# Moving the mask's rows head by head and exchanging two ScalarE operations in a fused attention and FFN kernel

## The chip, the cores and the metric

The kernel runs on one core of one Trainium2 chip. The metric is the device time of one launch in microseconds (us). A core has five engines that run their own instruction lists in order and wait for one another by semaphores: TensorE (PE in the profile; PEld is its weight load), VectorE (DVE), ScalarE (ACT), GpSimd (POOL) and SyncE (SP), which in this kernel issues nearly all DMA transfers. A DMA instruction waits on its issuing engine until its inputs are ready and its target is free, and all that stands behind it on that engine waits with it.

## The reference

Attention over 4 x 8 heads of 768 tokens with 64 values each, in which a query sees only the keys of its own hash bucket, and then a feed-forward layer with a rational function between its two products.

```python
q_bits = (einsum('bhsd,dk->bhsk', q, proj) > 0)      # 6 bits; k_bits likewise
mask = q_bucket[:, :, :, None] == k_bucket[:, :, None, :]
scores = where(mask, q @ k.T / sqrt(64), -1e9)
scores = scores - max(scores)
attn = exp(scores);  attn = attn / (sum(attn) + 1e-9)
x = (attn @ v), heads side by side                    # 3072 tokens x 512
h = x @ w_in                                          # 512 -> 2048
P = a0 + a1*h + a2*h*h + a3*h*h*h
Q = 1 + |b0|*|h| + |b1|*h*h
out = (P / (Q + 1e-6)) @ w_out                        # 2048 -> 512
```

All numbers are float32.

## The kernel before

The 32 heads are worked on as 16 pairs, p = 0 to 15. A pair has twelve score steps (two halves of 384 queries, six tiles of 128 keys), and each step makes the scores of both heads. The order of nearly all work on every engine comes from one list written by hand: `at(p, s, f, ...)` puts a call at place 12 * p + s, and the calls run in the order of their places. Below, **window w** is the stretch from place 12 * w to 12 * w + 12, in which pair w's scores are made, and "step s" is a place within it. While window w makes the scores of pair w, it also prepares pair w + 2 (its mask and its row maxima) and finishes pair w - 1.

What one window holds, as far as the change touches it:

- `scores` (one at each whole step): on the TensorE two matmuls for each head (`pss`), and on ScalarE one exponential for each head (`E<-pss`). The results stand in PSUM tiles that three buffers serve in turn, so the fourth tile of a row of scores can only be written when ScalarE has read the first.
- `values`: 24 matmuls for a half of a pair (`psv`), which sum into a PSUM tile of which there is one. `values_col` and `values_out` are the two ScalarE operations that read this tile (`col<-psv`, `xo<-psv,col`), and `values_store` is the DMA that puts the result into DRAM (`x_d<-xo`). For the second half of pair p they stand at steps 0.5, 1.5 and 3.0 of window p + 1.
- `high` and `low` split q and k of pair p into two parts on ScalarE and VectorE; `high_move` (step 1.9 of window p - 2, DMAs `q<-q` and `k<-k`) moves half of the first part to the other head's tile, and `second_high` (step 2.69) issues four more DMAs of the same names for pair p - 1.
- `bits` makes, for two pairs at once and in every even window, the rows that carry the bucket mask (`psb` on the TensorE, `mb<-psb` on VectorE); `penalties` scales them on ScalarE in place (`mb<-mb,cst`), at step 4.02.
- `maskrows` (step 4.03 of window p - 2) moves those rows by DMA into rows 64 to 76 of pair p's q and k tiles: `q<-mb` and `k<-mb` for head 0, then the same for head 1. For one of q's two tiles and one of k's, these are rows that `high_move` reads from, so the first of them has to wait for that DMA's end. In even windows it also waits for `penalties`.
- `maxstep` (twelve, from step 6.54 of window p - 2; `psm` on the TensorE, `m<-psm` on VectorE) makes the row maxima with those rows in the operands; the first six are head 0's. `shift_turn` (`pst`, `mt<-pst`) and `shift_rows` (`q<-mt`) turn the maxima into one more row of q.
- `load` (step 4.04) fetches q and k of a later pair (`qkf<-qT`, `qkf<-kT`, 384 KB each), and `weights` fetches and splits the FFN's weights (`wr<-w_in`, `wr<-w_out`, 512 KB each) along the way.

Window 0 has places of its own (the table `FIRST`): the mask's rows of pair 2 are moved at 8.2, both heads together, behind `penalties` at 7.315; the rows of the shift of pair 1 at 8.6 and 14.35; the load of pair 4 is at 7.35 (`load4`).

The FFN comes after the attention, from about 384 us on.

Of the kernel before, what the change touches and what calls it, by code (L numbers as in the profile page):

```python
# [21 lines left out]
NT = S // P  # L22
# [3 lines left out]
NPAIR = B * NHP  # L26
# [15 lines left out]
MID = dict(  # L42
    group=6, values=[0.66, 0.05], values_col=[1.5, 1.5], values_out=[2.5, 2.5],
    maxima=[6.54, 7.17, 8.32, 9.1, 10.1, 11.02, 12.25, 13.03, 14.15, 15.17, 16.01, 17.02], sums=17.05, sums_store=18.9,
    high=[-0.975, -0.974], low=[-0.946, 3.3, 3.35], bits=-0.945, penalties=4.02, high_move=1.9, maskrows=4.03, second_low=-2.2,
    second_high=2.69, load_v=10.99, shift_turn=5.67, shift_rows=8.82, load=4.04, recips=[23.5, 35.02, 35.3],
    weights=[[1.44, 5.01, 5.015, 5.06, 5.07, 5.08, 5.09, 5.3], [8.05, 11.005, 11.006, 11.022, 11.023, 11.024, 11.0255, 11.0256, 19.32, 21.22]],
    late_weights=[[1.44, 5.1, 5.11, 5.5, 5.65, 5.66, 11.02, 11.023], [8.05, 11.021, 11.022, 11.022, 11.024, 11.0245, 17.05, 17.665, 19.32, 21.22]],
    defer={5: 11.0252, 10: 17.1, 11: 17.2}, early_load=4.035, early_store=16.034, weights_last=[0.5, 0.8, 1.0, 1.2],
)  # L50

FIRST = dict(
    maxima1=[-0.072, -0.05, 5.52, 5.97, 6.42, 6.87, 7.32, 7.77, 8.22, 8.67, 9.12, 9.57], maxima2=9.5, rate2=0.82, high=[3.25, 3.53],
    low=[6.0, 6.05], bits=7.31, penalties=7.315, high_move=4.53, maskrows=8.2, second_low=-24.19, second_high=4.35, load_v=4.78, group=2,
    values=[-1.07, 2.65, 2.32, 2.35, 0.35, 0.61], values_out=3.02, high1=[-3.0, -3.2], low1=[-2.8, -2.95],
    high_move1=-2.7, load2=-2.6, load3=3.8, load4=7.35, penalties1=-24.26, maskrows1=-24.2,
    weights=[[-27.25, 5.45, 5.455, 6.9, 6.91, 7.317, 17.55, 18.3], [7.34, 9.04, 9.23, 9.24, 9.25, 9.26, 9.3, 11.9, 12.5, 46.81]],
    warm0=9, warm1=1, warm=3, warms=[3, 3, 3, 0, 1, 0], maxima00=[-4.3, -2.3, -4.2, -0.9, -1.2, -0.8], shift00=[-1.0, -0.2],
    shift0=[-0.08, -0.075], ahead=3, scores=[[-0.85, -0.4, -0.1], [0.1, 0.3, 0.4]], pen01=[-2.9, -0.35],
    second_high0=[-3.42, -3.4, -3.3, -3.25], load_v0=-3.3, bits1=-0.3, comp1=[-0.28, -0.27],  # L60
# [6 lines left out]
LAST = dict(  # L67
    group=6, values=[0.28, 0.44], values_out=0.46, vout14=[3.5, 3.03],
    hi14=17.05, weights15=[5.1, 5.11],
    tokens=[[-15.0, -11.5, -8.6, -4.9], [-7.43, -4.5, -2.83, -1.09], [1.1, 4.2, 5.45, 6.3]], terms=1.0, ffn=[13.61, 16.09, 16.14],  # L70
    sums=16.96, wide=8, share=6, third=0, sums14=14.69, weights14=-1.0, load_v=1.5, sumst14=22.46,
)
# [31 lines left out]
def move(nc, out, in_, queue=None):  # L104

    (queue or nc.sync).dma_start(out.bitcast(F32), in_.bitcast(F32))
# [72 lines left out]
def attention(ctx, tc, nc, raw, ps_b, tail, tokens, early, operands_to_terms, ffn, load, QF, KF, v, w_in, w_out, wo_d, ident, cst, ones, prj,  # L179
# [32 lines left out]
    Q1, Q2, K1, K2, LO, V, M, MB, ACC, EXP, AV, MS = ({} for _ in range(12))  # L212
# [51 lines left out]
        rows = MB[p + which[0]][0][sl]  # L264
        nc.scalar.activation(rows, rows.bitcast(F32), AF.Identity, scale=cst[sl, 1:2])

    def maskrows(p, queues=(None, None)):
        mb, o = MB.pop(p)
        for h in range(2):
            o1 = o + 14 * h  # L270
            move(nc, Q1[p][64:76, h, :], mb[o1 : o1 + 12].rearrange("p f c -> p (f c)"), queues[0])
            move(nc, K1[p][64:77, h, :], mb[o1 + 32 : o1 + 45].rearrange("p f c -> p (f c)"), queues[1])
# [228 lines left out]
    def at(p, s, f, *args):  # L501
        plan.setdefault(12 * p + s, []).append((f, args))
# [5 lines left out]
    for p in range(NPAIR):  # L508
        mid = 0 < p < NPAIR - 1
        n = MID["group"] if mid else (FIRST if p == 0 else LAST)["group"]  # L510
        for s in range(12):
            if p > 0 or s >= FIRST["ahead"]:
                at(p, FIRST["steps"].get(s, s) if p == 0 else s, scores, p, s)

            if p > 1:
                at(p - 2, FIRST["maxima2"] + FIRST["rate2"] * s if p == 2 else FIRST["third"] if p == 3 and s == 0 else MID["maxima"][s], maxstep, p, s, None, p == 2 or s not in MID["defer"])
                if p > 2 and s in MID["defer"]:
                    at(p - 2, MID["defer"][s], maxreduce, p, s)
            if s % n == n - 1:
                for i in range(s - n + 1, s + 1):  # L520
                    at(p, s + (MID["values"][s // n] if mid else (FIRST if p == 0 else LAST)["values"][s // n]), values, p, i)
            if s % NT == NT - 1 and mid and p < NPAIR - 2:
                at(p, s + MID["values_col"][s // n], values_col, p, s // NT)
            if s % NT == NT - 1:
                at(p, s + (LAST["vout14"][s // NT] if p == NPAIR - 2 else MID["values_out"][s // n] if mid else (FIRST if p == 0 else LAST)["values_out"]), values_out, p, s // NT)
        for hf in range(2):
            at(p, 6 * hf + 9, values_store, p, hf)
        if p < NPAIR - 1:
            at(p, MID["sums"] if p < NPAIR - 2 else LAST["sums14"], sums, p)
            at(p, MID["sums_store"] if p < NPAIR - 2 else LAST["sumst14"], sums_store, p)  # L530
        if p > 1:
            for t in range(2):
                at(p - 2, (MID if p > 2 else FIRST)["high"][t], high, p, t)
                at(p - 2, (MID if p > 3 else FIRST3)["low"][t + t * p % 2] if p > 2 else FIRST["low"][t], low, p, t, nc.vector if p > 3 else nc.gpsimd)
            if p % 2 == 0:
                at(p - 2, (MID if p > 2 else FIRST)["bits"], bits, p)
                at(p - 2, (MID if p > 2 else FIRST)["penalties"], penalties, p)
            at(p - 2, (MID if p > 2 else FIRST)["high_move"], high_move, p)
            at(p - 2, (MID if p > 2 else FIRST)["maskrows"], maskrows, p)
        if p > 0:  # L540
            at(p - 1, (MID if p > 1 else FIRST)["second_low"], second_low, p)
            at(p - 1, (MID if p > 1 else FIRST)["second_high"], second_high, p)
            at(p - 1, (LAST if p == NPAIR - 1 else MID if p > 1 else FIRST)["load_v"], load_v, p)
        if p > 1:
            at(p - 1, MID["shift_turn"] if p > 2 else FIRST["turn2"], shift_turn, p)
            at(p - 1, MID["shift_rows"], shift_rows, p)
        if p > 3:
            at(p - 4, MID["load"] if p > 4 else FIRST["load4"], load, p)
        if p % NHP == NHP - 1 and p + 1 < NPAIR:
            spread(p, MID["recips"], recips(p // NHP))  # L550
    for i in range(2 * NFC):
        o = 12 * (i // 2)
# [325 lines left out]
```

## Time and profile before

| | |
|---|---|
| time before, median of 3 runs | 913.45 us (912.49 to 915.35) |
| the profiled execution's own time | 913.39 us |
| its span, first to last instruction | 911.6 us |
| TensorE busy | 904.0 us (99%) |
| VectorE busy | 827.6 us (91%) |
| ScalarE busy | 649.6 us (71%) |
| GpSimd busy | 431.4 us (47%) |
| granted TensorE clock, mean | 1.000 |

The profiled execution lies 0.06 us below the median and has 1.8 us outside its span. Busy shares are means over the whole span; in the attention, the first 384 us, GpSimd is busy for most of the time, and after it for a fifth.

### The profile page before, as it was taken

The page shows a single profiled execution, that of the slowest core. Times are in us where ns is not written, and L with a number is a line of the kernel's source. Part 1 is how long each engine was busy: PE and PEld are TensorE (multiplying, and loading weights), DVE is VectorE, ACT ScalarE, POOL GpSimd, SP SyncE. Part 2 cuts the span into 40 slices and gives each one's busy share as a digit, 9 for nine tenths or more (in the row PEclk, how much of TensorE's full clock was granted, in tenths as well). Part 3 has the DMA queues.
Part 4 walks back from the last instruction along what each step waited for, and adds up shares of the span by engine and source line. Part 5 has one row for each costly group of instructions (what it writes and reads, how often), then busy time and mean ns, then how long its engine had stood idle before and what let it go on. Part 6 is the DMA issues. An engine that isn't in the chain of part 4 may idle for free.

```text
span 911.6 us, 13695 instructions
## 1 busy us (share of the span) xinstructions
PE 904.0 (99%) x4543; PEld 693.7 (76%) x4543; DVE 827.6 (91%) x1040; ACT 649.6 (71%) x1227; POOL 431.4 (47%) x411
## 2 busy tenths in 40 slices
PE   9999999999999999999999999999999999999998
PEld 5576767666767676678888888888888888888886
DVE  7888888888888888899999999999999989998997
ACT  7477777777777777787767666776677676767664
POOL 7697888787878886022222222222222222222221
PEclk9999999999999999999999999999999999999999
DMA  7878778888888778356104000400040012001001
GB/s 207 236 195 230 235 231 234 233 233 232 234 235 233 200 215 246 111 214 226 57 1 139 1 0 1 139 1 1 14 125 1 1 63 77 1 1 47 1 0 47
DMA packets 51243, 111.57 MB, mean 122 GB/s; under 512 B 9346, under 2 KB 20214, under 8 KB 51172
## 3 DMA queue, kind: packets, MB, share of 16 engines
q1 hardware_dynamic: 50740, 110.47, 41.0%
q8 instruction: 36, 0.59, 0.3%
q14 instruction: 35, 0.29, 0.1%
q10 hardware_dynamic: 432, 0.23, 0.1%
HBM read 56.82 MB, written 21.17 MB: 86 GB/s over the span
## 4 chain that ended last, share of the span: by engine, by line
PE 96%; DMA 1%; ACT 1%; DVE 1%; issue 0%; POOL 0%; SPq 0%; ACTq 0%; POOLq 0%; DVEq 0%
PE psh L99 29%; PE pso L99 29%; PE pss L99 15%; PE psv L99 13%; PE psm L99 7%; PE psb L99 1%; PE psu L99 1%; DMA q<-mb 1%; DVE m L99 0%; DMA k<-mb 0%; DMA qkf<-qT 0%; PE pst L99 0%; PE pst_None L99 0%; ACT E L99 0%; POOL lo L99 0%
## 5 line engine op out<-in xcount | busy, mean ns | idle before, releaser
L99 POOL TENSOR_TENSOR gl<-c,gh 128x512 fp32r<-128x512 f32 x95 | 136.9, 1441 | 408.0 <-ACT gh L99 398.0
L99 PE MATMUL pso<-wo,gh 128*128 128x512 f32 x768 | 235.8, 389 | 0.0
L99 POOL TENSOR_TENSOR acc<-acc,E 128x384 f32<-128x384 f32 x232 | 217.8, 976 | 8.4 <-ACT E L99 8.4
L99 ACT ACTIVATE E<-pss 128x384 f32<-128x384 f32 x384 | 167.9, 494 | 73.7 <-PE pss L99 62.0
L99 DVE TENSOR_REDUCE m<-psm 128x1 f32<-128x768 f32 x192 | 180.2, 954 | 27.0 <-PE psm L99 18.0
L99 PE MATMUL pss<-q,k 128*128 128x384 f32 (+2 forms) x768 | 170.8, 346 | 0.1
L99 PEld LDWEIGHTS pso<-wo,gh 128*128 128x128 f32 x768 | 144.0, 188 | 29.9 <-ACT o L99 0.2
L99 ACT ACTIVATE h<-psh 128x512 f32<-128x512 f32 x96 | 57.5, 599 | 133.3 <-PE psh L99 133.3
L99 PE MATMUL psh<-xh,wi_hi 128*128 128x512 f32 x384 | 149.6, 390 | 0.0
L99 PE MATMUL psh<-xh,wi_lo 128*128 128x512 f32 x384 | 149.4, 389 | 0.0
L99 PE MATMUL psh<-xl,wi_hi 128*128 128x512 f32 x384 | 149.4, 389 | 0.0
L99 PE MATMUL pso<-wo,gl 128*128 128x512 f32 x384 | 148.9, 389 | 0.0
L99 PEld LDWEIGHTS pss<-q,k 128*128 128x128 f32 (+2 forms) x768 | 133.9, 190 | 15.4 <-issue 8.2
L99 DVE SCALAR_TENSOR_TENSOR c<-c,ab,r 128x512 f32<-128x512 f32 x96 | 140.8, 1467 | 0.0
L99 PE MATMUL psv<-E,v 128*64 128x385 f32 x768 | 131.9, 492 | 0.0
L99 PEld LDWEIGHTS psv<-E,v 128*64 128x64 f32 x768 | 52.1, 137 | 70.7 <-issue 65.3
L99 PE MATMUL psm<-k,q 76*128 76x384 f32 (+1 forms) x384 | 100.3, 344 | 2.1 <-DMA k<-mb 0.7
L99 DVE SCALAR_TENSOR_TENSOR w<-h,absb,w 128x512 f32<-128x512 f32 x96 | 73.9, 769 | 16.6 <-ACT w L99 16.2
L99 PEld LDWEIGHTS psh<-xh,wi_hi 128*128 128x128 f32 x384 | 72.1, 188 | 16.1 <-ACT r L99 0.6
L99 PEld LDWEIGHTS pso<-wo,gl 128*128 128x128 f32 x384 | 72.1, 188 | 15.1
L99 PEld LDWEIGHTS psh<-xl,wi_hi 128*128 128x128 f32 x384 | 72.1, 188 | 14.9
L99 PEld LDWEIGHTS psh<-xh,wi_lo 128*128 128x128 f32 x384 | 72.0, 188 | 15.0
(89 smaller groups left out, 1168.0 us busy)
## 6 DMA issues: line engine op xcount, KB each, us to landing
q<-q SPq DMA_DIRECT2D x45, 192.0 KB
k<-k SPq DMA_DIRECT2D x45, 192.0 KB
wr<-w_in SPq DMA_DIRECT2D x16, 512.0 KB
wr<-w_out SPq DMA_DIRECT2D x16, 512.0 KB
wo_d<-wr SPq DMA_DIRECT2D x16, 512.0 KB
wo<-wo_d SPq DMA_DIRECT2D x16, 512.0 KB
qkf<-qT SPq DMA_DIRECT2D x16, 384.0 KB
qkf<-kT SPq DMA_DIRECT2D x16, 384.0 KB
```

The source lines that it names most:

```text
L99: return self.tc.keep_in_program_order(issue(*args, **kwargs))
```

## The change

- `maskrows` takes the heads that it is to move. For pairs 3 to 15 it is called twice in window p - 2: head 0 at step 2.7, head 1 at step 4.03. For pair 2 (window 0) it stays at 8.2 with both heads.
- `penalties` goes from step 4.02 to step 1.49, in windows 2, 4, 6, 8, 10 and 12.
- `values_out` of the second half of the odd pairs 1, 3, 5, 7, 9 and 11 goes from step 1.5 to step 4.02 of the next window, which is an even one, and its `values_store` from 3.0 to 4.028. So ScalarE exchanges two operations in windows 2 to 12 with even numbers. The odd windows keep both as they were.
- In window 0 the load of pair 4 goes from 7.35 to 8.65, behind the mask's rows of pair 2 (8.2) and the first rows of pair 1's shift (8.6).

On SyncE's queue the order of a window's middle was: two DMAs of `high_move`, four of `second_high`, `x_d<-xo`, four of `maskrows`, then loads. It becomes: `high_move`, `second_high`, two of `maskrows`, `x_d<-xo`, two of `maskrows`, then loads.

```diff
-    high=[-0.975, -0.974], low=[-0.946, 3.3, 3.35], bits=-0.945, penalties=4.02, high_move=1.9, maskrows=4.03, second_low=-2.2,
+    high=[-0.975, -0.974], low=[-0.946, 3.3, 3.35], bits=-0.945, penalties=1.49, odd_out=5.02, odd_store=16.028, high_move=1.9, maskrows=[2.7, 4.03], second_low=-2.2,
...
-    high_move1=-2.7, load2=-2.6, load3=3.8, load4=7.35, penalties1=-24.26, maskrows1=-24.2,
+    high_move1=-2.7, load2=-2.6, load3=3.8, load4=8.65, penalties1=-24.26, maskrows1=-24.2,
...
-    def maskrows(p, queues=(None, None)):
-        mb, o = MB.pop(p)
-        for h in range(2):
+    def maskrows(p, heads=(0, 1), queues=(None, None)):
+        mb, o = MB[p]
+        for h in heads:
             o1 = o + 14 * h
             move(nc, Q1[p][64:76, h, :], mb[o1 : o1 + 12].rearrange("p f c -> p (f c)"), queues[0])
             move(nc, K1[p][64:77, h, :], mb[o1 + 32 : o1 + 45].rearrange("p f c -> p (f c)"), queues[1])
...
-                at(p, s + (LAST["vout14"][s // NT] if p == NPAIR - 2 else MID["values_out"][s // n] if mid else (FIRST if p == 0 else LAST)["values_out"]), values_out, p, s // NT)
+                odd = s > NT and p % 2 == 1 and mid and p < NPAIR - 3
+                at(p, s + (MID["odd_out"] if odd else LAST["vout14"][s // NT] if p == NPAIR - 2 else MID["values_out"][s // n] if mid else (FIRST if p == 0 else LAST)["values_out"]), values_out, p, s // NT)
         for hf in range(2):
-            at(p, 6 * hf + 9, values_store, p, hf)
+            at(p, MID["odd_store"] if hf and p % 2 == 1 and mid and p < NPAIR - 3 else 6 * hf + 9, values_store, p, hf)
...
-            at(p - 2, (MID if p > 2 else FIRST)["maskrows"], maskrows, p)
+            if p > 2:
+                for h in range(2):
+                    at(p - 2, MID["maskrows"][h], maskrows, p, (h,))
+            else:
+                at(0, FIRST["maskrows"], maskrows, p)
```

## Rows read from the trace of the kernel before

**Rows 1.** The page of the profiled execution: its span, the first line of part 1 (busy time, share of the span and instructions of each engine) and the start of part 4 (the chain that ended last, share of the span by engine).

```profile
span 911.6 us, 13695 instructions
PE 904.0 (99%) x4543; PEld 693.7 (76%) x4543; DVE 827.6 (91%) x1040; ACT 649.6 (71%) x1227; POOL 431.4 (47%) x411
...
PE 96%; DMA 1%; ACT 1%; DVE 1%; issue 0%; POOL 0%; SPq 0%; ACTq 0%; POOLq 0%; DVEq 0%
```

**Rows 2.** Busy time of each engine in three stretches of the span. The columns are the stretch and its length in us, then PE, PEld, DVE, ACT and POOL with busy us and instructions, then the granted clock, the busy share of the DMA engines and the GB/s that they moved.

```profile
30.00:40.00 10.00, 9.49 (x58) 5.05 (x58) 9.94 (x14) 5.27 (x11) 5.11 (x6) 1.00 1.00 279
40.00:50.00 10.00, 9.28 (x52) 6.31 (x48) 8.68 (x12) 5.69 (x12) 5.66 (x6) 1.00 0.65 177
...
190.00:200.00 10.00, 9.54 (x59) 5.97 (x59) 7.71 (x11) 5.68 (x14) 8.23 (x9) 1.00 0.75 187
```

**Rows 3.** What the TensorE waited for in the whole span, three lines of seven (the other four, 2.5 us in all, lie in the first 32 us): engine and what it was to write, what it waited for, us in total, times, longest.

```profile
PE psm L99 <- DMA k<-mb: 0.7, 1, 0.7
...
PE psm L99 <- DMA q<-mb: 0.5, 1, 0.5
...
PE pst_None L99 <- DVE m L99: 0.2, 1, 0.2
```

**Rows 4.** Window 0, in order of time: start and length in us, engine, operation, out<-in, count, and in brackets the idle time before it and what ended it. First the TensorE, then ScalarE, then the DMA issues of SyncE's queue.

```profile
38.59 2.81 PE L99 MATMUL psv<-E,v 128*64 128x385 f32 x16
42.11 0.94 PE L99 MATMUL psm<-k,q 76*128 76x384 f32 x4 [0.72 <-DMA k<-mb]
...
34.68 0.94 ACT L99 ACTIVATE mb<-mb,cst 128x768 fp32r<-128x768 f32 x1 [3.69 <-DVE mb L99]
...
32.86 0.33 SPq L99 DMA_DIRECT2D qkf<-qT  x1
...
35.64 0.80 SPq L99 DMA_DIRECT2D q<-mb  x1
...
38.98 1.40 SPq L99 DMA_DIRECT2D q<-mt  x2
```

**Rows 5.** Window 7, the same view: SyncE's issues, then the TensorE; last, the stretch of the chain that ended last that answers to it (start, us, what).

```profile
185.54 0.47 SPq L99 DMA_DIRECT2D q<-q  x1
...
190.48 1.29 SPq L99 DMA_DIRECT2D x_d<-xo  x1
193.60 0.79 SPq L99 DMA_DIRECT2D q<-mb  x1
...
201.42 0.33 SPq L99 DMA_DIRECT2D x_d<-xo  x1
...
199.01 0.59 PE L99 MATMUL psm<-k,q 76*128 76x384 f32 x2 [0.46 <-DMA q<-mb]
...
193.60 5.11 DMA q<-mb
```

**Rows 6.** What SyncE's own queue waited for: the first line is from 190 to 194 us (window 7), the second from 121 to 126 us (window 4).

```profile
SPq L99 <- DMA q<-q: 1.8, 1, 1.8
...
SPq L99 <- DMA q<-q: 1.4, 1, 1.4
```

**Rows 7.** Window 4, in order of time: ScalarE with its six score steps, then the same stretch cut so that the first exponential of the third step stands alone, then the TensorE; last, VectorE's compare that makes the mask's rows.

```profile
120.86 0.59 ACT L99 ACTIVATE xo<-psv,col 128x384 f32<-128x384 f32 x1
121.32 2.78 ACT L99 ACTIVATE E<-pss 128x384 f32<-128x384 f32 x6
123.98 0.94 ACT L99 ACTIVATE mb<-mb,cst 128x768 fp32r<-128x768 f32 x1
124.81 0.87 ACT L99 ACTIVATE E<-pss 128x384 f32<-128x384 f32 x2
...
121.32 0.50 ACT L99 ACTIVATE E<-pss 128x384 f32<-128x384 f32 x1
...
120.19 0.51 PE L99 MATMUL psm<-k,q 76*128 76x384 f32 x2
...
121.60 0.90 PE L99 MATMUL pss<-q,k 77*128 77x384 f32 x4
...
122.33 0.51 PE L99 MATMUL psm<-k,q 76*128 76x384 f32 x2
...
125.66 0.54 PE L99 MATMUL psv<-E,v 128*64 128x385 f32 x2
...
118.51 1.01 DVE L99 TENSOR_SCALAR mb<-psb,cst 128x768 fp32r<-128x768 f32 x1
```

**Rows 8.** From the view by operation and shape: ScalarE's scaling of the mask's rows (busy us in all, mean ns of one | idle before).

```profile
L99 ACT ACTIVATE mb<-mb,cst 128x768 fp32r<-128x768 f32 x7 | 6.6, 936 | 3.7 <-DVE mb L99 3.7
```

**Rows 9.** Window 7 again, ScalarE and the TensorE at the third and fourth score step.

```profile
188.57 0.58 ACT L99 ACTIVATE xo<-psv,col 128x384 f32<-128x384 f32 x1
189.16 1.75 ACT L99 ACTIVATE E<-pss 128x384 f32<-128x384 f32 x4
...
189.34 0.99 PE L99 MATMUL pss<-q,k 77*128 77x384 f32 x4
```

**Rows 10.** Window 6, in order of time: two operations of VectorE, then one step of the TensorE.

```profile
160.03 0.69 DVE L99 TENSOR_SCALAR psx<-wr 128x512 int32<-128x512 int32 x1 [0.73 <-DMA wr<-w_out]
164.60 1.01 DVE L99 TENSOR_SCALAR mb<-psb,cst 128x768 fp32r<-128x768 f32 x1
...
165.77 0.52 PE L99 MATMUL psm<-k,q 76*128 76x384 f32 x2
```

## The prediction

> **What bounds the kernel.** I read the page first. TensorE is busy for 904.0 of 911.6 us, and 96% of the chain that ended last is its work [rows 1]. So the change can win only what TensorE stands idle, and it loses whatever new idle time it gives to TensorE. The busy time by stretches says where idle time is at all: in the attention most stretches of 10 us are full, and three that matter here are not: 30 to 40, 40 to 50 and 190 to 200 us, with 9.49, 9.28 and 9.54 us of work [rows 2]. The list of waits names the causes: 0.7 us for a transfer `k<-mb`, 0.5 us for a transfer `q<-mb`, both rows of the mask, and 0.2 us behind VectorE's maxima [rows 3]. The first lies at 42.11 us in window 0 [rows 4], the second at 199.01 us in window 7 [rows 5]. The other four waits lie before 32 us, where nothing is changed. Then I looked at ScalarE around the two operations that are exchanged, because ScalarE empties the score tiles that TensorE fills [rows 7].
>
> **Part 1, the load of pair 4 goes behind the shifts.** In window 0 the load is issued from 32.86 us, two transfers of 384 KB each, and the mask's rows from 35.64 us, as soon as `penalties` (34.68 + 0.94 = 35.62 us) is done; TensorE waits 0.72 us for the rows at 42.11 us [rows 4]. In that stretch all DMA engines are busy (share 1.00) and move 279 GB/s [rows 2], so the 786 KB ahead of the rows are worth about 2.8 us. The rows are issued at the same time as before, but they land up to 2.8 us sooner, and 0.72 us suffices. TensorE gains **0.72 us**; bounds 0 (the rows are late for another reason) and 0.72. The load itself is needed only at the end of window 1, 20 us later, and the next stretch has DMA time left (share 0.65) [rows 2], so I cost its delay at nothing; without that cover its 2.8 us would fall on the transfers of window 1.
>
> **Part 2, head 0's rows go two steps sooner.** In odd windows this does not send them much sooner. In window 7 SyncE had finished issuing at 190.48 + 1.29 = 191.77 us and then stood 1.8 us for `q<-q`, which is `high_move`, whose source the rows overwrite; the rows went at 193.60 us [rows 5, 6]. At step 2.7 they wait for the same landing. What changes is the order: the store `x_d<-xo` (192 KB) was issued ahead of them and is now behind. The rows took 5.11 us to land, and TensorE waited 0.46 us of that [rows 5]. At the 187 to 279 GB/s of such stretches [rows 2] 192 KB are worth 0.7 to 1.05 us, more than 0.46. So I count **0.46 us** gained, bounds 0 and 0.46.
>
> The price: the store's issue no longer lies in the shadow of that wait but between the two heads' rows, and head 1's rows, the loads and the weights of the window queue behind it. One such issue costs 0.33 us where the queue is free and 1.29 us where it is full [rows 5]; at its new place SyncE has just waited for a landing, so I take 0.33. Head 1's rows are needed six maxima later. The weights are nearer the edge: in window 6 VectorE waits 0.73 us for `wr<-w_out`, then works through to the compare `mb`, done at 164.60 + 1.01 = 165.61 us, and TensorE's second maxima at 165.77 us write the PSUM buffer which that compare has just left [rows 10]. Slack 0.16 us; 0.33 us of delay costs 0.17, rounded to **0.2 us** lost, bounds 0 and 1.29 - 0.16 = 1.13. In window 4 the same slack is larger: the compare ends at 118.51 + 1.01 = 119.52, the maxima start at 120.19 [rows 7], so 0.67 us cover the delay there.
>
> In even windows the rows had to wait for both `high_move` (1.4 us of SyncE's wait in window 4 [rows 6]) and `penalties` at 123.98 to 124.92 us [rows 7]. With `penalties` gone from there, they leave about 0.9 us sooner, and the store that now stands between them uses some of that up. TensorE waits for rows in no even window [rows 3], so this wins nothing.
>
> The Trainium skill, "DMA: Bandwidth & Descriptors", section on the anatomy of one DMA, speaks against moving a waiting transfer forward: DMA engines do not wait on semaphores, the issuing sequencer waits before it dispatches, so what is behind stands too. The trace agrees with it in the 1.8 us for which SyncE stood in window 7 [rows 6]; by this rule alone the part would cost its 0.2 us and win nothing, and the sum below would be 0.46 us higher.
>
> **Part 3, ScalarE's exchange.** The scaling of the rows takes 0.94 us (mean 936 ns over seven [rows 8]) and `xo` 0.59. By starts, the first holds ScalarE for 124.81 - 123.98 = 0.83 us and the second for 121.32 - 120.86 = 0.46 us [rows 7]. So in six windows (2, 4, ..., 12) the exponentials from the third step on start 0.37 us later, and those behind step 4.02 as before. The scaling needs the compare (119.52 us in window 4) at 120.86 us, 1.34 us later: no wait. `xo` at its new place would end at 123.98 + 0.59 = 124.57 us, and its PSUM tile is wanted by `psv` at 125.66 us [rows 7]: 1.09 us of cover.
>
> The lateness itself is not covered. Three PSUM buffers serve the score tiles, so head 1's tile of the fourth step (step 3) takes the buffer of head 0's third (step 2). Its first matmul is the third of four that start at 121.60 and take until 122.33, so it starts near 121.97; the exponential that frees the buffer ends at 121.32 + 0.50 = 121.82 [rows 7]. That is 0.15 us of slack against 0.37 us: TensorE would stand 0.22 us. Window 7 shows the same spot with a late exponential: there the third step's start came 0.59 us behind that of `xo` instead of 0.46, 0.13 us late, and the four matmuls took 0.99 us instead of 0.90 [rows 7, 9]. By this only 0.04 us were really free, and the stall would be 0.33. I take 0.30, nearer the row that shows a stall: 6 x 0.30 = **1.8 us** lost, bounds 6 x 0.22 = 1.3 and 6 x 0.37 = 2.2 (nothing at all is a rival below). It happens once a window: six exponentials take 2.78 us, 0.93 a step, and a step of TensorE takes (122.33 - 120.19) / 2 = 1.07 [rows 7], so ScalarE catches up. At its old place the scaling cost nothing, because 4 us of `psv` without any scores follow.
>
> **The sum**, against the profiled execution's 913.39 us: - 0.72 - 0.46 + 0.2 + 1.8 = + 0.82, that is 914.2 us; the median of the runs shown is 0.06 us above that execution, so **914.3 us**, 0.1% above the 913.45 before. A measurement of this kernel tells some 0.3% (2.7 us) from no change; the three runs before alone spread over 2.9 us.
>
> **Rivals.**
> - *The exchange is hidden.* If TensorE's order gives ScalarE its 0.37 us back (the slack at step 3 is larger than the rows say), only the gains stay, and the 0.17 us behind the maxima [rows 3] may go too: 913.45 - 0.72 - 0.46 - 0.17 = 912.1 us. For it: the slack is worked out from modelled ends of matmuls. Against it: the 0.99 us in window 7 [rows 9]. Chance 0.25.
> - *The rows land no sooner.* If what is late in windows 0 and 7 is not what stands ahead in the queue, both waits stay: 913.45 + 2.0 = 915.4 us. For it: around 199 us the DMA engines are not full on the mean (share 0.75 over that stretch [rows 2]). Against it: 5.11 us for 36 KB, right behind 192 KB. Chance 0.12. The Trainium skill, "DMA: Bandwidth & Descriptors", section "Queues, rings and completion order", states that completion is not in order for one issuing engine while each DMA engine takes its descriptors in ring order; by the second half the rows gain, by the first they need not, and no row here decides it.
> - *The store blocks SyncE.* If `x_d<-xo` takes the full queue's 1.29 us at its new place too, the weights of odd windows come 1.3 us later: window 6 stands 1.13 us, and five windows with window 4's slack 1.29 - 0.67 = 0.62 us each. With the exchange's 1.8 and the gains that is 913.45 - 1.18 + 1.8 + 1.13 + 3.1 = 918.3 us. It decides from an issue of about 0.7 us on. Against it: SyncE comes out of a wait. Chance 0.07.
> - *Nothing moves* (the exchange stalls and the gains cancel, or neither comes): 913.4 us. Chance 0.06.
>
> **How the numbers follow.** The forecast has 0.50. Its own bounds are 913.45 - 1.18 + 1.3 + 0 = 913.6 and 913.45 + 2.2 + 1.13 = 916.8 if every term is at its worst, which I cut to 916.2. The range reaches down to the first rival less the 0.2 us that such a sum can miss, 911.9. Faster than 910.7 needs idle time that TensorE does not have: 0.03. Slower than 916.2 is the third rival and the forecast's worst end: 0.09. The rest, 0.88, is no change.
>
> **What would show it.** Right: no wait of TensorE for `k<-mb` near 42 us and none for `q<-mb` near 199; at step 3 of windows 2 to 12 with even numbers, four `pss` matmuls of 1.15 to 1.25 us instead of 0.90, or a listed wait of 0.2 to 0.35 us on `E`; the mask's scaling right behind the second pair of exponentials. Wrong: those four matmuls still at 0.90; a wait of `psv` on `xo`; waits on `wr` in odd windows that grow by more than 0.5 us; or a wait for mask rows that stays.

## The result: 0.9% slower, by a wait that the sum did not have

| | kernel before | changed kernel |
|---|---|---|
| median of 20 runs each | 913.88 us (912.49 to 916.15) | 922.35 us (914.56 to 934.13) |
| ratio, with its 95% interval | | 1.0086 (1.0072 to 1.0100) |
| profiled execution, its span | 913.39 us, 911.6 us | 926.06 us, 924.3 us |

The forecast was 914.3 us, range 911.9 to 916.2. The ratios here and below leave out runs more than 1.5% above the fastest of their kernel: three of the changed kernel's twenty, those above 930 us, and one of without_load. Without those three the changed kernel still scatters over 12.6 us (914.56 to 927.12), where the one before scatters over 3.7. All fences below are of the changed kernel unless said otherwise. First the page (span, busy time, granted clock in 40 slices), then what TensorE waited for over 0.3 us in all, then busy time by stretches (columns as in [rows 2]).

```profile
span 924.3 us, 13691 instructions
...
PE 911.1 (99%) x4543; PEld 698.0 (76%) x4543; DVE 828.3 (90%) x1040; ACT 651.6 (70%) x1227; POOL 431.5 (47%) x411
...
PEclk9997999999999999999999999999999999999999
```
```profile
PE psm L99 <- DVE mb L99: 6.0, 2, 5.2
PE psw L99 <- DVE hs L99: 1.3, 1, 1.3
PE pst_None L99 <- DVE m L99: 0.4, 1, 0.4
PE psm L99 <- DVE k L99: 0.4, 2, 0.2
```
```profile
40.00:50.00 10.00, 10.00 (x56) 6.67 (x51) 9.41 (x13) 6.49 (x13) 5.46 (x6) 1.00 0.72 203
70.00:80.00 10.00, 4.90 (x36) 2.57 (x32) 10.00 (x6) 3.14 (x8) 8.31 (x10) 0.89 0.94 236
80.00:90.00 10.00, 9.90 (x34) 8.38 (x34) 6.25 (x8) 6.48 (x12) 7.38 (x8) 0.50 0.15 43
...
190.00:200.00 10.00, 10.00 (x58) 7.30 (x57) 8.73 (x11) 8.24 (x19) 9.78 (x10) 1.00 0.60 178
```

The two waits for rows that were to go are gone: neither `k<-mb` nor `q<-mb` is in the list [rows 3], and the stretches at 40 and 190 us, at 9.28 and 9.54 before [rows 2], are full. What is new lies between 70 and 92 us, in window 2: TensorE works 4.90 us of ten and then runs at a granted clock of 0.50, the 1.2 GHz level. In order of time (start and length in us, engine, operation, count, idle time before it and what ended it), TensorE, VectorE, ScalarE and GpSimd:

```profile
74.01 0.88 PE L99 MATMUL pss<-q,k 77*128 77x384 f32 x4
80.10 1.01 PE L99 MATMUL psm<-k,q 76*128 76x384 f32 x2 [5.21 <-DVE mb L99]
80.91 1.48 PE L99 MATMUL pss<-q,k 77*128 77x384 f32 x4
...
90.16 4.76 PE L99 MATMUL psv<-E,v 128*64 128x385 f32 x24
```
```profile
71.85 7.28 DVE L99 TENSOR_TENSOR lo<-qkf,q 128x768 fp32r<-128x768 f32 x1
79.04 1.00 DVE L99 TENSOR_SCALAR mb<-psb,cst 128x768 fp32r<-128x768 f32 x1
```
```profile
80.08 0.94 ACT L99 ACTIVATE mb<-mb,cst 128x768 fp32r<-128x768 f32 x1 [4.58 <-DMA q<-q]
```
```profile
53.36 1.84 POOL L99 TENSOR_TENSOR lo<-qkf,q 128x768 fp32r<-128x768 f32 x1 [5.10 <-DMA ab<-coef]
...
69.21 7.20 POOL L99 TENSOR_TENSOR acc<-acc,E 128x384 f32<-128x384 f32 x8
76.36 1.95 POOL L99 TENSOR_TENSOR acc<-E,E 128x384 f32<-128x384 f32 x2
82.48 8.05 POOL L99 TENSOR_TENSOR acc<-acc,E 128x384 f32<-128x384 f32 x8 [4.17 <-ACT E L99]
```

Read from the bottom: GpSimd works from 53.36 to 78.31 us without a pause, from 57 us on almost only at adding up exponentials (`acc`, function `scores`). In that time VectorE starts pair 4's low part `lo<-qkf,q` (function `low`: an input minus its rounded copy, both in SBUF), and it lasts 7.28 us, until 79.13 us. The compare `mb` stands behind it on VectorE, TensorE needs the PSUM buffer that the compare reads and waits 5.21 us, and then four score matmuls take 1.48 us instead of 0.86 to 0.90. The same places in the kernel before:

```profile
48.92 1.84 POOL L99 TENSOR_TENSOR lo<-qkf,q 128x768 fp32r<-128x768 f32 x1 [0.78 <-DMA q<-lo]
...
75.05 1.98 POOL L99 TENSOR_TENSOR acc<-E,E 128x384 f32<-128x384 f32 x2 [3.03 <-ACT E L99]
```
```profile
71.09 1.75 DVE L99 TENSOR_TENSOR lo<-qkf,q 128x768 fp32r<-128x768 f32 x1
72.86 1.02 DVE L99 TENSOR_SCALAR mb<-psb,cst 128x768 fp32r<-128x768 f32 x1
```
```profile
74.58 0.52 PE L99 MATMUL psm<-k,q 76*128 76x384 f32 x2
...
80.08 4.10 PE L99 MATMUL psv<-E,v 128*64 128x385 f32 x24
```

There GpSimd's own low part starts 4.4 us sooner, GpSimd pauses 3.03 us from 72.02 us, and VectorE's low part is through at 72.84. TensorE reaches the `psv` of window 2 at 80.08 us before and 90.16 us after: 10.1 of the 12.7 us by which the spans differ. 5.5 of them lie ahead of the second maxima (74.58 against 80.10), the other 4.6 are the half clock's.

### The profile page after: what moved, and what is told of

Read it like the earlier page. It is cut to its first block, busy times and chain, and to the rows that moved or that the text cites. A ratio compares the mean times of both kernels' runs of the same rounds, so it can differ in the third digit from the quotient of the medians.

```text
span 924.3 us, 13691 instructions
## 1 busy us (share of the span) xinstructions
PE 911.1 (99%) x4543; PEld 698.0 (76%) x4543; DVE 828.3 (90%) x1040; ACT 651.6 (70%) x1227; POOL 431.5 (47%) x411
## 4 chain that ended last, share of the span: by engine, by line
PE 94%; DVE 2%; DMA 2%; ACT 1%; issue 0%; SPq 0%; POOL 0%; DVEq 0%; ACTq 0%
PE psh L99 28%; PE pso L99 28%; PE pss L99 14%; PE psv L99 13%; PE psm L99 7%; PE psu L99 1%; DVE lo L99 1%; PE psb L99 1%; DVE m L99 1%; DMA q<-q 1%; DMA v<-v 0%; DMA prj<-proj 0%; ACT E L99 0%; SPq L99 0%; POOL acc L99 0%
## 5 line engine op out<-in xcount | busy, mean ns | idle before, releaser
L99 POOL TENSOR_TENSOR acc<-acc,E 128x384 f32<-128x384 f32 x232 | 219.2, 983 | 12.9 <-ACT E L99 12.7
L99 PE MATMUL pss<-q,k 128*128 128x384 f32 (+2 forms) x768 | 173.6, 349 | 0.4
L99 PEld LDWEIGHTS pss<-q,k 128*128 128x128 f32 (+2 forms) x768 | 136.4, 192 | 16.0 <-issue 8.2
L99 DVE SCALAR_TENSOR_TENSOR c<-c,ab,r 128x512 f32<-128x512 f32 x96 | 138.6, 1444 | 0.0
L99 PE MATMUL psm<-k,q 76*128 76x384 f32 (+1 forms) x384 | 102.6, 350 | 6.7 <-DVE mb L99 6.0
```

The costliest lines, as they stand in the source:

```text
L99: return self.tc.keep_in_program_order(issue(*args, **kwargs))
```

## The experiments

The **port theory**: a low part on VectorE cannot run while GpSimd is in an instruction that reads SBUF; it must get its turn between two of them, and with GpSimd behind by 4.4 us there is no pause in window 2. The load, now ahead of pair 2's `q<-lo` and `k<-lo`, makes GpSimd late, because GpSimd's low part of pair 3 overwrites what these transfers read. (At 53.36 us the bracket names another transfer, `ab<-coef`. But that low part also waits for the semaphores of both `q<-lo`, and the later of these completes at 53.20 us, in the kernel before at 48.76; GpSimd starts 0.16 us behind it each time.) The rivals are the **exchange** (ScalarE's `mb` now stands ahead of the exponentials and holds them up behind the late compare) and the late transfers themselves. Each kernel was timed in five rounds beside the kernel before, whose medians were 913.26 to 913.79 us. Diffs show only the entries that change.

| run | median (range), us | ratio to before (95%) |
|---|---|---|
| load_alone | 918.26 (913.65 to 921.96) | 1.0040 (1.0020 to 1.0060) |
| without_load | 915.75 (913.68 to 931.20) | 1.0023 (1.0012 to 1.0033) |
| load_behind_lows | 914.40 (913.22 to 925.72) | 1.0031 (1.0007 to 1.0055) |
| late_gpsimd | 925.11 (924.26 to 925.95) | 1.0132 (1.0118 to 1.0145) |
| sums_left_out | 914.54 (912.56 to 920.91) | 1.0014 (1.0000 to 1.0028) |
| low4_on_gpsimd | 926.08 (921.03 to 933.54) | 1.0152 (1.0124 to 1.0179) |
| load_low4 | 926.15 (921.24 to 926.54) | 1.0122 (1.0102 to 1.0143) |
| acc_both | 915.17 (913.96 to 916.32) | 1.0014 (1.0005 to 1.0023) |
| exchange_alone | 914.25 (912.82 to 915.31) | 1.0009 (1.0000 to 1.0018) |
| rows_odd | 915.76 (913.67 to 924.51) | 1.0032 (1.0011 to 1.0053) |
| lows_rows_odd | 914.18 (913.28 to 920.80) | 1.0022 (1.0007 to 1.0037) |
| load_behind_alone | 913.97 (912.81 to 914.83) | 0.9998 (0.9989 to 1.0007) |
| load_behind_rows | 913.75 (912.28 to 915.41) | 1.0000 (0.9991 to 1.0009) |

### The load alone, and the change without it

```diff
 load_alone, from the kernel before
-load4=7.35
+load4=8.65
 without_load, from the changed kernel
-load4=8.65
+load4=7.35
```


> The kernel before with the load of pair 4 at 8.65 instead of 7.35, and nothing else. The port theory: the load now stands ahead of the transfers of pair 2's low parts, GpSimd's low parts of pair 3 start near 53 us instead of 49, its chain of accumulations runs without a pause through the end of window 1, VectorE's low part of pair 4 (two inputs in SBUF, about 72 us) finds GpSimd busy and takes 5 us or more instead of 1.75, TensorE waits several us for the compare that stands behind it and then runs for some 10 us at a granted clock near 0.5: a median of 917 to 925 us, scattered by over 3 us, with no wait of 0.72 us for the rows at 42 us. The exchange theory (ScalarE stands behind the late compare, and that makes the stall): without the exchange the stall stays under 2 us and no slice falls to 0.5: 912.5 to 915 us. My recorded sum: 912.7 us.

> The changed kernel with the load of pair 4 back at 7.35: rows and exchange alone. The port theory: GpSimd's low parts of pair 3 start near 49 us, VectorE's low part near 72 us takes under 2 us, no stall near 80 us, clock 1.0; what is left is the exchange's small stalls at the fourth step of five or six even windows (0.26 us each, 1.3 to 1.6) less 0.46 at 199 us: 913.9 to 915.5 us. The exchange theory: a stall at the start of window 2 stays and the time is 917 us or more. My recorded sum: 915.0 us.

The load alone makes the stall without the exchange: VectorE's low part takes 4.67 us beside a GpSimd that works through to 74.25 us, and TensorE's clock falls (granted clock 0.52 from 76 to 86 us). It does not do so each time: four of the nine executions took 913.65 to 914.93 us at a mean clock of 0.999 or more. GpSimd, VectorE, TensorE:

```profile
67.06 7.19 POOL L99 TENSOR_TENSOR acc<-acc,E 128x384 f32<-128x384 f32 x8
```
```profile
70.40 4.67 DVE L99 TENSOR_TENSOR lo<-qkf,q 128x768 fp32r<-128x768 f32 x1
```
```profile
76.05 0.80 PE L99 MATMUL psm<-k,q 76*128 76x384 f32 x2 [1.99 <-DVE mb L99]
76.65 1.48 PE L99 MATMUL pss<-q,k 77*128 77x384 f32 x4
```

Without the load window 2 is clean, as expected, but the time is not: 915.75 us. The profiled execution, the one left out of the ratio, took 931.20 us and shows two stalls. One is the same thing again, with the other low part, in window 10 and with no load near (GpSimd, VectorE, TensorE):

```profile
267.18 7.18 POOL L99 TENSOR_TENSOR acc<-acc,E 128x384 f32<-128x384 f32 x8
```
```profile
268.92 6.26 DVE L99 TENSOR_TENSOR lo<-qkf,k 128x768 fp32r<-128x768 f32 x1
```
```profile
279.19 0.28 PE L99 MATMUL pst_None<-cst,m 128*12 128x128 f32 x1 [4.27 <-DVE m L99]
...
281.24 1.48 PE L99 MATMUL pss<-q,k 77*128 77x384 f32 x4
```

The other has no lost turn in it: the low part before it took 0.95 us. VectorE had waited 3.10 us for weights, the compare came late, TensorE stood only 0.82 us, and then its granted clock was 0.50 from 215 to 225 us (VectorE, then TensorE):

```profile
208.99 0.69 DVE L99 TENSOR_SCALAR psx<-wr 128x512 int32<-128x512 int32 x1 [3.10 <-DMA wr<-w_out]
```
```profile
214.63 0.96 PE L99 MATMUL psm<-k,q 76*128 76x384 f32 x2 [0.82 <-DVE mb L99]
215.38 1.48 PE L99 MATMUL pss<-q,k 77*128 77x384 f32 x4
```

So the load is the main cause and not the only one. The turn can be lost wherever a low part meets GpSimd at work, and a compare that late weights hold up can bring the clock down by itself. How often either happens in the executions without a trace is not shown.

### The load behind the low parts' transfers

```diff
 load_behind_lows, from the changed kernel
-load4=8.65
+load4=9.9
```


> The changed kernel with the load of pair 4 at 9.9, behind the transfers of pair 2's low parts instead of ahead of them. The port theory: those transfers land before 51 us again, GpSimd starts its low parts near 49 us, the low part near 72 us takes under 2 us, no stall near 80 us: 913 to 915.5 us, close to the changed kernel without the load's move less up to 0.7 us for the rows at 42 us; a new wait for the transfers that now stand behind the load (high parts of pair 3, near 56 to 60 us) would show as 1 to 3 us more. If any later load brings the stall (a rival): as the changed kernel, 918 us or more.

914.40 us, as the port theory has it: GpSimd is not late, and the low part near 71 us took 1.65 us. Two of eleven executions were still above 917 us.

### GpSimd made late, with nothing else touched

```diff
 late_gpsimd, from the kernel before, in low()
-engine.tensor_tensor(out=LO[p, t], ...)
+for _ in range(4 if (p, t) == (3, 0) else 1):
+    engine.tensor_tensor(out=LO[p, t], ...)
```


> The kernel before, with GpSimd's low part of pair 3 for q computed four times instead of once (5.5 us more work for GpSimd near 50 us, nothing else touched: no transfer, no order of ScalarE or SyncE). The port theory: GpSimd's accumulations run into window 2 without a pause, VectorE's low part near 71 us takes 3 us or more in many executions, TensorE stalls behind the compare and the granted clock falls: 915 to 922 us, scattered by over 3 us. Rival (transfers or the exchange are the cause): 913 to 914.5 us, as before, low part at 1 to 2 us.

925.11 us, above what the port theory gave and with no execution below 924. No transfer and no order of ScalarE was changed, so GpSimd's lateness suffices. VectorE, GpSimd, TensorE:

```profile
72.04 9.36 DVE L99 TENSOR_TENSOR lo<-qkf,q 128x768 fp32r<-128x768 f32 x1
```
```profile
78.64 1.94 POOL L99 TENSOR_TENSOR acc<-E,E 128x384 f32<-128x384 f32 x2
```
```profile
82.38 1.01 PE L99 MATMUL psm<-k,q 76*128 76x384 f32 x2 [6.70 <-DVE mb L99]
```

### GpSimd's sums left out

```diff
 sums_left_out, from the changed kernel, in scores()
+if p > 0 and late < LAST["share"]:
+    if kt % n == 1:
+        engine.memset(acc[:, h, :], 1.0)
+    continue
 engine.tensor_tensor(out=acc[:, h, :], ...)
```


> The changed kernel without GpSimd's accumulations of the exponentials from pair 1 on (they are left out, and each sum is a constant that GpSimd writes without reading), this time with an edit that takes effect: 108 instructions fewer on GpSimd. The load of pair 4 still stands ahead of pair 2's low parts. The port theory: every low part on VectorE takes 0.95 us in every window, no wait for the compare above 1 us, clock 1.0 throughout, hardly any scatter: 911.5 to 914.8 us, with the exchange's small stalls left. Rival (the low part near 72 us waits for the transfers that read its buffer, late by the load): it still takes 4 us or more there, TensorE stalls and the clock falls: 917 us or more.

914.54 us. The low parts' durations (min/median/max in ns, first and last start):

```profile
L99 DVE TENSOR_TENSOR lo<-qkf,q x12: 937/948/967, 71.1 to 325.8; 128x768 fp32r<-128x768 f32 x12
L99 DVE TENSOR_TENSOR lo<-qkf,k x12: 948/948/950, 78.5 to 331.5; 128x768 fp32r<-128x768 f32 x12
```

In the kernel before the twelve for q had a median of 1800 ns and in the changed kernel a longest of 7275. The late transfers are still there (GpSimd's low part of pair 3 starts at 51.70 us), so the second rival falls. GpSimd is idle beside the low parts here, so whether its reads or any work of it would do is not told apart. One execution took 920.91 us at a mean clock of 0.994; what happened in it no trace shows, but a stall behind late weights, as in without_load, needs no sums.

An earlier edit for this (no_sums) had a condition that never held, so its instructions were those of the changed kernel. It stands as a second sample of that: 919.43 us (915.30 to 925.67), ratio 1.0078 (1.0047 to 1.0108), low part near 70 us at 3.93 us.

> The changed kernel without GpSimd's accumulations of the exponentials from pair 1 on (they are left out, and each sum is a constant that GpSimd writes without reading), so that GpSimd is idle beside VectorE's low parts; the load of pair 4 still stands ahead of pair 2's low parts. The port theory: every low part on VectorE takes 0.95 us in every window, no wait for the compare above 1 us, clock 1.0 throughout, hardly any scatter: 911.5 to 914.5 us, with the exchange's small stalls left. Rival (the low part near 72 us waits for the transfers that read its buffer, late by the load): it still takes 4 us or more there, TensorE stalls and the clock falls: 917 us or more.

### The harmed instruction moved to GpSimd

```diff
 low4_on_gpsimd, from the changed kernel; load_low4, from the kernel before with load4=8.65
-nc.vector if p > 3 else nc.gpsimd
+nc.vector if p > 4 or p == 4 and t else nc.gpsimd
```


> The changed kernel with one instruction moved: pair 4's low part for q goes from VectorE to GpSimd, where it stands in line among the accumulations (1.84 us). The port theory: no VectorE instruction near 72 us asks for what GpSimd holds, the compare is done by 74 us, no stall of TensorE over 1 us there, clock 1.0 in most executions: 914 to 915.5 us, and single executions above 917 only where another window's low part loses its turn. Rival (the late transfers, the late rows or ScalarE's order make the stall): it stays, 918 us or more.

> The kernel before with the load of pair 4 at 8.65 and pair 4's low part for q on GpSimd: part 1 with the instruction that it harmed taken out of GpSimd's way. The port theory: TensorE keeps the 0.72 us of the rows at 42 us and pays nothing near 80 us: 912.5 to 913.3 us, little scatter, against 918.3 for the load alone. Rival: as the load alone, 917 us or more.

Both missed: 926.08 and 926.15 us. The first half of the expectation came true, the compare is done at 73.57 us and nothing waits for it. But GpSimd, with 1.87 us more to do, is now busy through the next low part, that for k, and TensorE waits there instead. In low4_on_gpsimd, GpSimd, VectorE, TensorE:

```profile
74.33 1.87 POOL L99 TENSOR_TENSOR lo<-qkf,q 128x768 fp32r<-128x768 f32 x1
...
78.09 7.20 POOL L99 TENSOR_TENSOR acc<-acc,E 128x384 f32<-128x384 f32 x8
```
```profile
72.55 1.02 DVE L99 TENSOR_SCALAR mb<-psb,cst 128x768 fp32r<-128x768 f32 x1 [1.69 <-PE psb L99]
...
78.19 7.91 DVE L99 TENSOR_TENSOR lo<-qkf,k 128x768 fp32r<-128x768 f32 x1
```
```profile
90.12 0.38 PE L99 MATMUL pst_None<-cst,m 128*12 128x128 f32 x1 [5.92 <-DVE m L99]
```

The stall went with the collision, not with the instruction: for the port theory, against my reading that one low part was the trouble.

### Half as many instructions on GpSimd

```diff
 acc_both, from the changed kernel, in scores(), pairs from 1 on
-for h in heads:
-    engine.tensor_tensor(out=acc[:, h, :], in0=x[:, h, 0:HQ], in1=e[:, h, 0:HQ], op=ALU.add)
+engine.tensor_tensor(out=acc, in0=x[:, :, 0:HQ], in1=e[:, :, 0:HQ], op=ALU.add)
```


> The changed kernel with GpSimd's two accumulations of a step (one for each head) in one instruction: the same work in half as many instructions, each of about 1.75 us instead of two of 0.87, and each waits for the second head's exponentials. If the turn is lost only by asking in the last 0.3 us of a GpSimd instruction, it is lost half as often, but GpSimd is as late in window 2: 915 to 920 us, with more executions below 916 than the changed kernel had (1 of 20), and low parts of up to 2.7 us where the turn is won. Rival (VectorE waits for any pause of GpSimd, however many instructions): as the changed kernel, 919 to 925 us.

915.17 us with no execution above 916.32, the low end of what I expected and well under the rival: the changed kernel's scatter is gone, and no low part for q took over 2.08 us (the durations as above).

```profile
L99 DVE TENSOR_TENSOR lo<-qkf,q x12: 943/1996/2083, 71.0 to 325.7; 128x768 fp32r<-128x768 f32 x12
```

GpSimd was also 2 us less late here (its low part of pair 3 starts at 51.41 us), so fewer instructions and less lateness are not told apart.

### The exchange alone

```diff
 exchange_alone, from the kernel before
-penalties=4.02
+penalties=1.49, odd_out=5.02, odd_store=16.028
```


> The kernel before with ScalarE's exchange and the store that goes with it, rows and load at their old places. My recorded term: six stalls of 0.30 us, 915.2 us in the undisturbed executions. As the changed kernel's trace shows it: four or five stalls of 0.26 us, 914.5 to 915. The exchange hidden: 913.5. The port theory adds: where the times of VectorE's low parts against GpSimd's have shifted in the even windows, one of them can lose its turn in some executions, which then take 3 to 15 us more.

914.25 us, 0.8 us over the kernel before by the ratio, where I had 1.8. The stall at the fourth step is there at its forecast size, in all six windows (four `pss` of 1.23 to 1.25 us), but part of it comes back (TensorE in window 4; the four `pss` took 0.90 us before [rows 7]):

```profile
121.65 1.25 PE L99 MATMUL pss<-q,k 77*128 77x384 f32 x4
...
130.14 0.95 PE L99 MATMUL pss<-q,k 77*128 77x384 f32 x4
```

In the kernel before, the step that 130.14 answers to is this one:

```profile
129.72 1.09 PE L99 MATMUL pss<-q,k 77*128 77x384 f32 x4
```

0.35 us lost and 0.14 us regained, where the window's second half had stood a little already.

### The rows alone, and both gains without the exchange

```diff
 rows_odd, from the kernel before: head 0 at 2.7 in odd windows, 4.03 in even ones
-at(p - 2, (MID if p > 2 else FIRST)["maskrows"], maskrows, p)
+for h in range(2):   # p > 2; maskrows=[2.7, 4.03]
+    at(p - 2, MID["maskrows"][h if p % 2 else 1], maskrows, p, (h,))
 lows_rows_odd: the same, and load4=9.9
```


> The kernel before with head 0's rows two steps sooner in odd windows alone, nothing else: part 2 by itself as far as it can stand without the exchange. My recorded terms: 913.45 - 0.46 + 0.2 = 913.2 us, no wait for rows at 199 us. As the run with the load behind the low parts suggests: the wait for rows goes, but waits of 0.5 to 0.7 us of TensorE behind VectorE's late weights come in one to three odd or following even windows: 913.5 to 914.8 us.

> The kernel before with the load of pair 4 at 9.9 (behind the transfers of pair 2's low parts) and head 0's rows two steps sooner in odd windows alone, ScalarE as before: the two gains of the recorded sum without its loss. The sum: 913.45 - 0.72 - 0.46 + 0.2 = 912.4 us; no wait for rows at 42 and 199 us, no long low part near 72 us. Rival (the load disturbs whatever it stands ahead of): a new wait of 0.5 us or more between 50 and 90 us, 913.5 to 916 us.

Neither gained: 915.76 and 914.18 us, both slower than the kernel before, with intervals clear of 1. The wait for rows at 199 us is gone in both, but further on VectorE waits longer for its weights, and TensorE for VectorE. In lows_rows_odd, VectorE, then TensorE:

```profile
240.64 0.69 DVE L99 TENSOR_SCALAR psx<-wr 128x512 int32<-128x512 int32 x1 [1.07 <-DMA wr<-w_in]
```
```profile
244.74 0.28 PE L99 MATMUL pst_None<-cst,m 128*12 128x128 f32 x1 [0.66 <-DVE m L99]
```

That the store's new place makes this wait is not shown: load_behind_rows, below, leaves rows and store where they were, and has the same two waits there, 1.16 us of VectorE and 0.76 us of TensorE. Both traces here are of executions near 914 us; what the slow ones stood for (three of twelve above 917 us in rows_odd, two of twelve in lows_rows_odd) no trace shows.

Another attempt (without_exchange) had the rows at 2.7 in even windows too, ahead of the scaling at 4.02, which leaves the scaling out of head 0's rows there. ScalarE's scaling then waited for transfers that read what it overwrites (17.7 us in five waits) and the time was 970.40 us. It says nothing of its question, only that the rows can't go sooner in even windows without the exchange.

> The changed kernel with ScalarE's two operations and the store back at their old places: load and rows alone. The port theory: GpSimd's chain is as late as in the changed kernel, VectorE's low part near 72 us is held up as long, TensorE stalls near 78 us and the clock falls: 917 to 925 us. The exchange theory: the exponentials of window 2 no longer stand behind the compare, TensorE stalls under 2 us, no slice near 0.5: 912 to 914.5 us. My recorded sum: 912.4 us.

### The load's gain by itself

```diff
 load_behind_alone and load_behind_rows, from the kernel before
-load4=7.35
+load4=9.9
 ...
+load4=16.035
```


> The kernel before with the load of pair 4 at 9.9, behind the transfers of pair 2's low parts, and nothing else. The port theory: GpSimd is not delayed, VectorE's low part near 71 us takes under 2.2 us, and the 0.72 us of TensorE's wait for rows at 42 us is won: 912.5 to 913.2 us, with as little scatter as the kernel before. Rival (a load at any later place than before disturbs what comes next): 914 us or more, or single executions above 917.

> The kernel before with the load of pair 4 at 16.035, right behind the mask's rows of pair 3 in window 1, and nothing else. If only what the load stands ahead of decides: no wait for rows at 42 us and none near 61 us, low part near 71 us under 2.2 us, 912.6 to 913.3 us, 0.5 us below the kernel before. Rival (the load is then too late for its own use, ScalarE's rounding near 68 us, or pair 5's load and the weights behind it are): a wait of 1 us or more between 65 and 95 us, 914 us or more, or single executions above 917.

No loss, no scatter, and no gain: 0.9998 and 1.0000, where I expected some 0.5 us. In the first TensorE lost what it had won to the next rows, those of pair 3 (load_behind_alone, TensorE in order of time):

```profile
60.76 0.59 PE L99 MATMUL psm<-k,q 76*128 76x384 f32 x2 [0.66 <-DMA k<-mb]
```

In the second neither wait is there and the median still does not move. The 0.72 us was also no fixed sum: in rows_odd, where window 0 is untouched, the stretch from 40 to 50 us is full. Nor was the 0.46 us of window 7: TensorE does not wait for rows there in load_alone, load_behind_alone and load_behind_rows, though none of them moves the rows, and in acc_both, which does, part of the wait stays:

```profile
199.40 0.59 PE L99 MATMUL psm<-k,q 76*128 76x384 f32 x2 [0.31 <-DMA q<-mb]
```

No version beat the kernel before.

## Why the prediction was wrong

- **Part 1, the gain: the wait went, its 0.72 us won nothing.** TensorE no longer waits at 42 us, as forecast, but no run kept the time (load_behind_alone, load_behind_rows).
- **Part 1, "I cost its delay at nothing": the step that failed.** I looked whether the load itself was needed later and whether DMA time was left, and put a price of 2.8 us "on the transfers of window 1" if the cover went. I did not ask which transfers these were and who waited for them. They were `q<-lo` and `k<-lo`, GpSimd waited for them, and GpSimd's pause in window 2 was what let VectorE's low part through. load_alone shows the load enough to cause it, late_gpsimd GpSimd's lateness, sums_left_out that without GpSimd's sums it does not occur. No term of the sum, and none of the four rivals, asked what GpSimd shares with VectorE.
- **Part 2: the gain not shown, the price too small.** The sum had 0.26 us won; rows_odd lost 2.5 us of median. (lows_rows_odd, with part 1's gain in the sum, was to win 0.98 and lost 0.9.) The wait at 199 us went in the changed kernel, but it also went where the rows were not moved, and 0.31 us of it stayed in acc_both. So the rival that the rows land no sooner is not decided, and neither is what I had drawn from the Trainium skill ("DMA: Bandwidth & Descriptors", section on the anatomy of one DMA), that nothing would be won: the rows were issued no sooner (193.83 us in rows_odd against 193.60 [rows 5]), and no run shows that the store behind them made them land sooner. The rival of a blocked SyncE came true in part. The store's issue at its new place cost 0.34 to 0.52 us in eleven windows of the changed kernel, but 0.77 in one and 1.39 in window 5, and one window on VectorE waits 2.19 us for `wr<-w_out` where it waited 0.73 [rows 10], and TensorE 0.83 us; the rival had 1.13 there (the changed kernel, SyncE, VectorE, TensorE):

```profile
160.03 1.39 SPq L99 DMA_DIRECT2D x_d<-xo  x1
```
```profile
172.31 0.69 DVE L99 TENSOR_SCALAR psx<-wr 128x512 int32<-128x512 int32 x1 [2.19 <-DMA wr<-w_out]
```
```profile
177.94 0.62 PE L99 MATMUL psm<-k,q 76*128 76x384 f32 x2 [0.83 <-DVE mb L99]
```

  That stall is not tied to the store alone: load_low4, with store and rows at their old places, has 0.82 us at the same step, and sums_left_out too, with a store issue of 0.51 us. That so short a stall can cost the clock as well, as in without_load, no term had.

- **Part 3: mechanism and place right, size wrong.** 1.8 us forecast, 0.8 measured, because part of each stall comes back in the same window. As a sum the undisturbed terms were near: with the turn mostly not lost, the change costs 1.3 us (acc_both, sums_left_out), where I had 0.8.
- **The exchange as an aggravation stays open.** The load alone costs 4.8 us and the whole change 8.5. That ScalarE's `mb` holds the exponentials back behind the late compare can be read at 80.08 us, but no run here separates it from the later GpSimd of the changed kernel (53.36 us against 51.18 in load_alone). Nor do the times ask for it: the three parts alone cost 0.40, 0.32 and 0.09%, together 0.81 of the whole change's 0.86%.

## What to carry to other kernels

When a transfer is moved back, list every transfer that it now stands ahead of, and follow the engine that waits for each to its next pause: a pause of an engine off the critical path can be what another engine lives on. Where VectorE has two inputs in SBUF beside a GpSimd that is nearly full, look at the spread of that instruction's durations and not at its mean; one that is always 0.9 to 1.9 us may have been lucky in its schedule. Count the clock with every stall of TensorE: in two executions here it cost some 5 us more, after 0.82 us as after 5.21 us. And a wait that is seen in one trace is no fixed sum that its removal gives back; see first whether it stands in other executions of the same kernel or of near ones.

## What the runs showed of the hardware

**VectorE's two-input instructions take turns with GpSimd, and can lose many in a row.** With GpSimd idle a low part takes 0.95 us. In five stalls above it ended a constant time after GpSimd's last instruction before a pause: 79.13 - 78.31, 75.07 - 74.25, 275.18 - 274.36 and 81.40 - 80.58 are 0.82 us each, 86.10 - 85.29 is 0.81. In the traces of both kernels and of twelve runs (all but acc_both, sums_left_out and without_exchange), 290 low parts began during a GpSimd instruction; 206 ended within 1 us of that instruction's end, and of the other 84 all but two ended at a pause of GpSimd of 0.5 us or more, past one to nine more instructions. What decides the first turn is not settled. Of the 175 that came over 0.33 us ahead of the instruction's end 171 got it, of the 115 that came later 35; but three of the seven waits of more than 3 us had come 0.48 to 0.94 us ahead. The Trainium skill, "SBUF — State Buffer", section "Who interferes with whom", states that a VectorE instruction with two SBUF inputs contends with a GpSimd instruction that reads SBUF, and that issue order decides who blocks. The trace agrees with the contention: 0.95 us with GpSimd idle, 7.28 us beside its sums. By start times it does not bear out the order: 84 of the 290 did not get the next turn, and here the measurement decides. The page would have put the low parts on the list of what part 1 had to ask about.

**TensorE's clock fell to its lower level after stalls of 0.8 to 6.7 us, but not after every short one.** After 5.21 us (the changed kernel) the granted clock was 0.50 from 80 to 90 us, after 6.70 us (late_gpsimd) 0.50 from 82 to 92 us, after 1.99 us (load_alone) 0.52 from 76 to 86 us, and four `pss` took 1.48 or 1.49 us instead of 0.87. In without_load it fell after 0.82 us; after 0.82 or 0.83 us in the changed kernel (177.94 us), acc_both, sums_left_out and load_low4 it stayed at 1.00. What tells these apart no run shows. The loss did not grow with the stall. From the last `psv` before it to the next one it was 18.75 us in without_load, 19.34 in load_alone and 22.78 in the changed kernel, each time against 12.85 in the kernel before: 5.1, 4.5 and 4.7 us beyond stalls of 0.82, 1.99 and 5.21 us. After 1.24 us (no_sums; granted clock 0.66 from 75 to 80 us) it was 1.7 us. In the changed kernel the lower level lasted into the `psv` at 90.16, whose 24 matmuls still took 4.76 us instead of 4.10.
